# Two layers of attention and routed feed-forward on one core: sixteen small stores become one, and the order inside the row-maximum pairs

## The chip, the cores and the metric

The kernel runs on one core of a Trainium2 chip. The metric is the device time of one execution in microseconds (us). The kernel before took 4527.57 us, the median of three runs (4526.86 to 4528.15). A profile of one further execution stands beside them. In it the engines are called PE (matrix products), PEld (its weight loads), DVE (vector operations), ACT (activations), POOL (a second elementwise engine) and SP, whose queue issues most of the transfers between the chip's memory and the core's own.

## The reference

Two layers are applied twice in turn: full attention with 32 heads on 2048 rows of width 1024, then a feed-forward block that only the 8 rows with the highest router score pass through.

```python
def _A_ref(x, wqkv, wo):
    H = 32; Dh = D // H
    q, k, v = ...                       # x @ wqkv, split into heads of 32 columns
    scores = jnp.einsum("bhqd,bhkd->bhqk", q, k) * Dh ** -0.5
    p = _softmax(scores, axis=-1)
    o = jnp.einsum("bhqk,bhkd->bhqd", p, v)
    return o... @ wo

def _B_ref(x, w_r, w_gate, w_up, w_down):
    r = x @ w_r
    idx = jnp.argsort(-r, axis=-1)[:, :8]
    ...                                 # silu(x_sel @ w_gate) * (x_sel @ w_up) @ w_down, scaled by sigmoid(r_sel)
    return x + upd                      # the chosen rows are added back

x = A_x
x = x + _A_ref(_layernorm(x), A_wqkv, A_wo)
x = x + _B_ref(_layernorm(x), B_w_r, B_w_gate, B_w_up, B_w_down)
x = x + _A_ref(_layernorm(x), A_wqkv, A_wo)
x = x + _B_ref(_layernorm(x), B_w_r, B_w_gate, B_w_up, B_w_down)
```

The change lies in the softmax of the attention: in its row maxima and in its row sums.

## The kernel before, in words

Each layer has a stage of projections, an attention stage, and a stage with the output projection and the feed-forward block. The attention stage is cut into 32 *units*: 8 groups of 4 heads, and for each group 4 chunks of 512 queries (`QC`, line 23). A unit has 16 *steps*, one for each tile of 128 keys, so a layer's attention stage has 512 steps. The order of every engine's instructions is the order of the code (`manual_schedule`, line 101); only waits are put in by the builder.

**One step** (the loop at line 1298) issues on PE, in this order: the first pair of row-maximum products for a later unit (`pre_pair` with k = 0, line 1318), the score products of two head pairs (`scores`, line 775; ACT turns each result into exponentials at line 1260), the second pair (`pre_pair` with k = 1, line 1325), and the product of the step before with the values (`pv_step`, line 1154).

**Row maxima.** The softmax needs the maximum of each row ahead of its unit, so the products for it run 25 steps early (`LEAD`): step s works on row block s + 25. For a block, `pre_pair` forms products with four stretches of 512 keys in two pairs. Two heads lie in the two halves of the array's rows, so the two products of a pair, b = 0 and b = 1, go to different halves and to different PSUM banks `ps[0]` and `ps[1]`. They come from a pool of three banks (`ps_st`, line 108), out of which the row sums and their totals take a bank too. `jj`, the lowest bit of the block's number, says which of the two heads is done with *paired keys*: for that head the first product (k = 0) is with differences of keys (`DT`, read as `dt` in the profile), ACT keeps the positive part of it (line 739), and the second product (k = 1) is added and the maximum taken in one operation on DVE (line 741), so that one reduction covers 1024 keys. The other product of each pair, with plain keys, is reduced alone on DVE (line 743). `jj` changes from step to step: in one step the product with paired keys is b = 0, in the next b = 1. The products are issued with b = 0 first in both.

**Row sums.** The exponentials of the 16 key tiles of a unit are added up, partly by transfers that accumulate (line 1194), partly by POOL (line 1164). What is left is summed over the 128 rows in two ways. `sum_out` (line 1218) uses products with ones for the tiles named `DIRECT` and stores four rows (`sd`). For the accumulated rest, `turn` (line 1166) transposes 32-by-32 blocks and reduces them into a small tile `FOLD`, in eight operations spread over steps 8 to 15 of the next unit. Once in four units, in step 15, `total` (line 1179) adds the four partition groups with one product, transposes the result and stores it to the memory tensor `sd2` (called `se` in the profile). `sum_load` (line 1224) reads both tensors at the end of the layer. The last three units of a layer are not turned; their places in `sd2` are filled once, at the stage's start, by three stores of zeros (line 1253).

**The queue.** All loads and stores of this stage but the accumulating ones are issued by SP in the order of the code (`dma`, line 103, called from line 105 in the profile). After `total` of step 15 come, in steps 0 to 5 of the next unit: the store of the last unit's output (`oT`, line 1210, after DVE's copy at line 1208) and six query loads for the unit after next (`load_q`, line 703), one a step. The first four (`q<-qh`) carry what the row-maximum products read; these begin on that unit in step 7. After them come the stores of `sum_out` and, in two units of four, the keys of the next group. Three query tiles take turns.

Of the kernel before, what the change touches and what calls it, by code (L numbers as in the profile page):

```python
# [8 lines left out]
F32 = mybir.dt.float32  # L9
# [4 lines left out]
OP = mybir.AluOpType  # L14
AX = mybir.AxisListType
# [6 lines left out]
NG = H // 4  # L22
QC = 4
# [29 lines left out]
TURNED = NU - 3  # L53
# [23 lines left out]
def tile_kernel(ctx, tc, x, wqkv, wo, w_r, w_gate, w_up, w_down, out):  # L77
    nc = tc.nc
    sync, dve, act, pool, pe = nc.sync, nc.vector, nc.scalar, nc.gpsimd, nc.tensor
# [23 lines left out]
    def dma(out, in_):  # L103
        f = [a.bitcast(F32) if a.dtype == F32R else a for a in (out, in_)]
        sync.dma_start(f[0], f[1])  # L105

    def ps_st():
        return banks["now"][1].tile([128, 512], F32, name="st", bufs=1 if banks["wide"] else 3)

    def ps_pre():  # L110
        return psum.tile([128, 1024], F32, name="pre", bufs=2)

    def ps_pv():
        return psum.tile([128, 512], F32, name="pv")
# [12 lines left out]
    lanes = cons.tile([128, 32], F32, name="lanes")  # L127
# [540 lines left out]
    def layer(n, src, dst, prev=None, following=None):  # L668
# [7 lines left out]
        sd2 = dram.tile([NT, 4, NG, 128], F32, name=f"se{n}")  # L676
# [7 lines left out]
        KS, Q, V, NM, QP, DT = {}, {}, {}, {}, [], {}  # L684
# [27 lines left out]
        def half(h, slot):  # L712
            return slice(64 * (h % 2), 64 * (h % 2) + SLOT_ROWS[slot])

        def load_d(g, b, i):
            dma(DT[g % 2][64 * b:64 * b + 32, i, :].rearrange("p (c k) -> p c k", c=2),
                kd[g, 2 * b:2 * b + 2, 64 * i + 32 * b:64 * i + 32 * b + 32, :].rearrange("c p k -> p c k"))

        def pre_pair(u, r, k, side):

            qt, rest = divmod(r, 4)
            i, jj = divmod(rest, 2)
            g = u // QC
            if u not in NM:
                NM[u] = small.tile([128, 4, 4, 4], F32, name="nm", bufs=3)
            ps = [ps_st(), ps_st()]
            for b in range(2):
                rows, p = half(b, 0), ps[b]
                if b != jj:
                    keys = KS[g % 2][rows, i, 0, (2 * jj + k) * 512:(2 * jj + k + 1) * 512]  # L730
                elif k == 0:
                    keys = DT[g % 2][rows, i, :]
                else:
                    keys = KS[g % 2][rows, i, 0, jj * 1024:(jj + 1) * 1024].rearrange("p (c k) -> p c k", c=2)[:, :, 256:512]
                    p = p.rearrange("p (c k) -> p c k", c=2)
                pe.matmul(p, Q[u][rows, i, 0, qt * 128:(qt + 1) * 128], keys, start=True, stop=True, tile_position=(64 * b, 0))  # L736
            h = 2 * i + jj
            if k == 0:
                act.activation(side, ps[jj], AF.Relu)  # L739
            else:  # L740
                dve.tensor_tensor_reduce(side, ps[jj], side, 1.0, -3.0e38, OP.add, OP.max, NM[u][:, 0, h, qt:qt + 1])  # L741
            h = 2 * i + 1 - jj
            dve.tensor_reduce(NM[u][:, 1 + k, h, qt:qt + 1], ps[1 - jj], axis=AX.X, op=OP.max)  # L743
# [58 lines left out]
        with ExitStack() as pst:  # L802
# [249 lines left out]
            for k, (c, wb, i) in enumerate(steps):  # L1052
                b = k % 24
# [18 lines left out]
                j = k // 2 + 1  # L1072
# [7 lines left out]
                t = 4 * (c + 1) + at // 4  # L1080
# [41 lines left out]
        with sbuf(f"at{n}", bufs=2) as aw:  # L1122
# [5 lines left out]
            P, PV, ACC, TURN, FOLD = {}, {}, {}, {}, {}  # L1128
# [37 lines left out]
            def turn(u, k):  # L1166
                h, back = divmod(k, 2)
                if not back:
                    TURN[u] = aw.tile([128, 512], F32, name="turned", bufs=1)
                    dve.transpose(TURN[u], ACC[u][:, 512 * h:512 * h + 512])  # L1170
                    return
                if u % QC == 0 and h == 0:
                    FOLD[u // QC] = aw.tile([128, 4, 64], F32, name="fold", bufs=1)
                dve.tensor_reduce(FOLD[u // QC][:, u % QC, 16 * h:16 * h + 16], TURN.pop(u).rearrange("p (a c) -> p a c", c=32),
                                  axis=AX.X, op=OP.add)
                if h == 3:
                    ACC.pop(u)

            def total(u):
                if u % QC != QC - 1 and u != TURNED - 1:  # L1180
                    return
                g, m = u // QC, u % QC + 1
                p = ps_st()[0:32, 0:64 * m]
                pe.matmul(p, lanes, FOLD.pop(g)[:, 0:m, :].rearrange("p q c -> p (q c)"), start=True, stop=True, tile_position=(0, 0))
                t = aw.tile([128, 512], F32, name="sm", bufs=1)[0:32, 0:64 * m]
                dve.transpose(t, p)
                for q in range(m):
                    for h in range(4):
                        r = 16 * (h % 2)
                        dma(sd2[4 * q:4 * q + 4, h, g, :].rearrange("t (c r) -> t c r", r=32),  # L1190
                            t[r:r + 16, 64 * q + 32 * (h // 2):64 * q + 32 * (h // 2) + 32])

            def merge(u, a, b):
                pool.dma_start(P[u * NT + a], P[u * NT + b], accum_op=OP.add)  # L1194
# [33 lines left out]
            def recip(t, i):  # L1228
# [3 lines left out]
                dma(half_of(rd, i), t)  # L1232

            fns = {"add": acc_add, "merge": merge, "sum": sum_out, "turn": turn, "total": total}

            def emit(s, where):
# [13 lines left out]
            for i in range(2):  # L1250
                for b in range(2):
                    load_d(0, b, i)
            for t in range(TURNED % QC, QC):
                dma(sd2[4 * t:4 * t + 4, :, NG - 1, :].rearrange("t h c -> (t h) c"), DT[0][32:48, 0, 0:128])
            wop = None
            def half_step(s, i, third=False):
                if i == 0:
# [40 lines left out]
            for s in [*range(threes), *range(threes, NS, 3), *range(NS, NS + 14)]:  # L1298
# [14 lines left out]
                if pr:  # L1313
                    side = aw.tile([128, 512], F32, name="first", bufs=1) if s % NT != 1 or pr[0] >= PLAIN else None
                    if pr[0] < PLAIN:
                        pre_mm(*pr, 0, False, side=side)
                    else:
                        pre_pair(*pr, 0, side)
# [3 lines left out]
                if pr and pr[0] < PLAIN:  # L1322
                    pre_mm(*pr, 1, False)
                elif pr:
                    pre_pair(*pr, 1, side)
                t = s - 1 if s < NS - LEAD else s - 2
# [18 lines left out]
        if True:  # L1345
# [81 lines left out]
            for t in range(NT - 2 if n else NT):  # L1427
                oh, ol = OT.pop(t)
                p = ps_pre()
# [7 lines left out]
                if True:  # L1437
                    for k, l, r, a in products:
                        if first_stage and k == 2 and (t - CT, a) in ((0, 7), (1, 0), (1, 6), (2, 0), (2, 6), (3, 0)):
                            next(first_stage, None)  # L1440
                        for bl in halves:
                            pe.matmul(p[:, bl], l[:, a, :], r[a][:, bl], start=(k == 0 and a == 0),  # L1442
                                      stop=(k == 2 and a == KD - 1))
# [47 lines left out]
        if n:  # L1491
# [3 lines left out]
            p = [[waste[:, h] for h in halves], [ps_st(), ps_pv()]]  # L1495
# [72 lines left out]
            for i in range(2):  # L1568
                t = NT - 2 + i
# [11 lines left out]

    x3 = tuple(dram.tile([rows, D], F32, name=f"x3{i}") for i, rows in enumerate((CUT + 8, S - CUT)))
    list(layer(0, x, x3, following=lambda ffn: layer(1, x3, out, prev=ffn)))


# [24 lines left out]
```

## Time and profile before

| | |
|---|---|
| median of three runs | 4527.57 us |
| profiled execution | 4530.56 us |
| its span, first to last instruction | 4528.8 us |
| mean granted PE clock | 0.982 |
| busy PE, DVE, ACT, POOL | 97%, 68%, 63%, 72% |
| stores `se<-sm` of the turned sums | 232, 2 KB each |
| row-maximum products (line 736) | 2880 with plain keys, 960 with paired keys |

Busy time is the union of an engine's instructions; PE's ends are modelled, so a busy PE is not PE at its peak. A row of a time table has the start in us from the span's start, the length in us from the first to the last of the instructions merged into it, the engine, the line, the operation, and what it writes and reads; in brackets stands the idle time ahead of it and what ended it. "SPq" and the like are the queue of an engine, which issues transfers and waits.

### The profile page before, as it was taken

The page shows a single profiled execution, that of the slowest core. Times are in us where ns is not written, and L with a number is a line of the kernel's source. Part 1 is how long each engine was busy: PE and PEld are TensorE (multiplying, and loading weights), DVE is VectorE, ACT ScalarE, POOL GpSimd, SP SyncE. Part 2 cuts the span into 40 slices and gives each one's busy share as a digit, 9 for nine tenths or more (in the row PEclk, how much of TensorE's full clock was granted, in tenths as well). Part 3 has the DMA queues.
Part 4 walks back from the last instruction along what each step waited for, and adds up shares of the span by engine and source line. Part 5 has one row for each costly group of instructions (what it writes and reads, how often), then busy time and mean ns, then how long its engine had stood idle before and what let it go on. Part 6 is the DMA issues. An engine that isn't in the chain of part 4 may idle for free.

```text
span 4528.8 us, 75535 instructions
## 1 busy us (share of the span) xinstructions
PE 4383.9 (97%) x28255; PEld 2646.1 (58%) x28255; DVE 3059.5 (68%) x5605; ACT 2867.5 (63%) x3447; POOL 3268.6 (72%) x1367
## 2 busy tenths in 40 slices
PE   9999999999999999999999999999999999999998
PEld 7888755445445454458877786545454454544584
DVE  3322588778878787786522226878787888887863
ACT  3322299889888888870222223989898898988600
POOL 5554399889899898835634443989898898988252
PEclk9999999999999999999999999999999999999999
DMA  6977498888898988769699774988988888887698
GB/s 222 271 242 225 134 200 190 178 187 187 177 199 173 196 185 179 165 161 248 182 312 314 251 211 135 197 186 185 195 186 178 185 186 185 191 178 158 167 284 329
DMA packets 366189, 918.69 MB, mean 203 GB/s; under 512 B 52700, under 2 KB 188476, under 8 KB 309486
## 3 DMA queue, kind: packets, MB, share of 16 engines
q0 software_dynamic: 53312, 384.39, 42.7%
q1 hardware_dynamic: 295198, 490.07, 35.8%
q10 hardware_dynamic: 17312, 39.40, 3.0%
q8 instruction: 222, 3.64, 0.3%
q14 instruction: 145, 1.19, 0.1%
HBM read 395.35 MB, written 134.67 MB: 117 GB/s over the span
## 4 chain that ended last, share of the span: by engine, by line
PE 88%; DMA 6%; DVE 2%; issue 1%; SPq 1%; POOL 1%; ACT 0%; POOLq 0%; ACTq 0%; DVEq 0%
PE pv L1154 22%; PE pre L775 21%; PE st L932 16%; PE st L736 15%; PE pre L932 6%; PE pre L1442 5%; DMA q<-qh 2%; SPq L105 1%; PE st L1203 1%; DMA wraw<-in_A_wqkv_dram 1%; PE pre L757 1%; PE pv L932 1%; DMA ord<-rd 0%; PE pv L567 0%; PE third L775 0%
## 5 line engine op out<-in xcount | busy, mean ns | idle before, releaser
L1164 POOL TENSOR_TENSOR acc<-acc,P 128x2048 f32<-128x2048 f32 x420 | 2054.6, 4892 | 9.4
L1260 ACT ACTIVATE P<-pre 128x1024 f32<-128x1024 f32 x2016 | 1954.9, 1023 | 25.6 <-PE pre L775 23.8
L743 DVE TENSOR_REDUCE nm<-st 128x1 f32<-128x512 f32 x1920 | 1320.8, 688 | 159.9 <-PE st L736 134.7
L775 PE MATMUL pre<-q,ks 64*128 64x512 f32 (+1 forms) x8064 | 1136.4, 397 | 1.7 <-ACT P L1260 1.7
L1154 PE MATMUL pv<-P,v 128*32 128x512 f32 x8192 | 1097.6, 610 | 0.3 <-DMA v<-vd 0.3
L736 PE MATMUL st<-ks,q 64*128 64x512 f32 x2880 | 929.3, 451 | 0.1
L775 PEld LDWEIGHTS pre<-q,ks 64*128 64x128 f32 (+1 forms) x8064 | 779.2, 188 | 162.6 <-ACT P L1260 27.8
L741 DVE CUSTOM_DVE_ANT_0 first<-st,first 128x512 f32<-128x512 f32 x960 | 664.1, 692 | 304.2 <-PE st L736 278.2
L739 ACT ACTIVATE first<-st 128x512 f32<-128x512 f32 x960 | 575.9, 600 | 382.0 <-PE st L736 379.6
L736 PEld LDWEIGHTS st<-ks,q 64*128 64x128 f32 x2880 | 515.3, 186 | 474.1 <-DVE nm L741 375.8
L736 PE MATMUL st<-dt,q 64*128 64x512 f32 x960 | 481.6, 502 | 111.1 <-DMA q<-qh 86.9
L1194 POOL DMA_DIRECT2D P<-P x366 | 367.5, 1004 | 297.9 <-PE st L736 223.7
L736 PEld LDWEIGHTS st<-dt,q 64*128 64x128 f32 x960 | 177.2, 185 | 515.0 <-ACT P L1260 340.4
L947 DVE TENSOR_TENSOR lo<-st,hi 128x512 fp32r<-128x512 f32 x128 | 88.4, 691 | 511.3 <-ACT hi L946 453.1
L832 POOL TENSOR_TENSOR ohl<-wraw,ord 128x2048 fp32r<-128x2048 f32 (+1 forms) x54 | 222.3, 4122 | 242.2 <-ACT ord L827 211.5
L946 ACT CAST hi<-st 128x512 fp32r<-128x512 f32 x128 | 75.3, 588 | 441.2 <-PE st L932 347.3
L832 POOL TENSOR_TENSOR wl<-wraw,wh 128x2048 fp32r<-128x2048 f32 (+1 forms) x54 | 223.1, 4134 | 171.4 <-ACT wh L831 153.8
L1154 PEld LDWEIGHTS pv<-P,v 128*32 128x32 f32 x8192 | 163.9, 108 | 267.8 <-issue 261.1
L1164 POOL TENSOR_TENSOR acc<-P 128x2048 f32<-128x2048 f32 x62 | 311.6, 5026 | 0.1
L181 POOL TENSOR_TENSOR rs<-mv,eps_c 128x1 f32<-128x1 f32 x64 | 26.8, 419 | 288.1 <-DVE mv L179 288.1
L1442 PE MATMUL pre<-woh,ohl 128*128 128x512 f32 x960 | 223.9, 390 | 2.8 <-DVE pre L1476 1.9
L1373 ACT CAST ohl<-ord 128x1024 fp32r<-128x1024 f32 x32 | 33.6, 1051 | 273.7 <-DMA ord<-rd 93.6
(421 smaller groups left out, 5311.6 us busy)
## 6 DMA issues: line engine op xcount, KB each, us to landing
P<-P POOLq DMA_DIRECT2D x366, 1024.0 KB, 9.1
wraw<-in_A_wqkv_dram SPq DMA_DIRECT2D x96, 1024.0 KB
q<-qh SPq DMA_DIRECT2D x256, 128.0 KB
ks<-kh SPq DMA_DIRECT2D x112, 256.0 KB
fw<-in_B_w_down_dram SPq DMA_DIRECT2D x17, 1024.0 KB
vd<-vn SPq DMA_DIRECT2D x32, 512.0 KB
qh<-hi SPq DMA_DIRECT2D x64, 256.0 KB
ql<-lo SPq DMA_DIRECT2D x64, 256.0 KB
```

Source lines behind the costliest of these rows:

```text
L736: pe.matmul(p, Q[u][rows, i, 0, qt * 128:(qt + 1) * 128], keys, start=True, stop=True, tile_position=(64 * b, 0))
L739: act.activation(side, ps[jj], AF.Relu)
L741: dve.tensor_tensor_reduce(side, ps[jj], side, 1.0, -3.0e38, OP.add, OP.max, NM[u][:, 0, h, qt:qt + 1])
L743: dve.tensor_reduce(NM[u][:, 1 + k, h, qt:qt + 1], ps[1 - jj], axis=AX.X, op=OP.max)
L775: pe.matmul(p[:, b * 512:(b + 1) * 512], KS[(u // QC) % 2][rows, i, slot, kt * 128:(kt + 1) * 128], Q[u][rows, i, slot, :], start=(slot == ...
L832: pool.tensor_tensor(wl[:, sl], raw[:, sl], wh[:, sl].bitcast(F32), op=OP.subtract)
L932: pe.matmul(p, *pair(a, l, r), start=(a == 0 and k == 0), stop=(a == KD - 1 and k == 2))
L1154: pe.matmul(PV[u][32 * h:32 * h + 32, :], V[g, kt // 4][:, kt % 4, 32 * h:32 * h + 32], P[s][:, h, :], start=(kt == 0), stop=(kt == NT - 1 ...
L1164: (dve if on_dve else pool).tensor_tensor(o, a, P[u * NT + k].rearrange("p h c -> p (h c)"), op=OP.add)
L1194: pool.dma_start(P[u * NT + a], P[u * NT + b], accum_op=OP.add)
L1260: act.activation(P[s][:, 2 * i:2 * i + 2, :].rearrange("p h c -> p (h c)"), p, AF.Exp, scale=SCALE)
L1442: pe.matmul(p[:, bl], l[:, a, :], r[a][:, bl], start=(k == 0 and a == 0), stop=(k == 2 and a == KD - 1))
```

## The change

In `pre_pair` the two products of a pair are issued in the order `jj`, `1 - jj`: the product with paired keys first. Nothing else of the function changes; where `jj` is 0 the order is what it was.

For the turned sums, `FOLD` becomes a tile of 256 columns in another order, into which the reduction writes with a stride, so that after the total and its transposition each of 32 rows holds two pieces of 128 sums as they lie in memory. `total` then stores the sums of four units with one transfer of 32 rows by 2 pieces of 512 bytes in place of sixteen of 16 rows by 128 bytes. The last total of a layer, which has one unit, also takes all 256 columns; the fold tile of that group is set to zero first, and the three stores of zeros at the start of the stage go.

```diff
-            for b in range(2):
+            for b in (jj, 1 - jj):
                 rows, p = half(b, 0), ps[b]
...
                 if u % QC == 0 and h == 0:
-                    FOLD[u // QC] = aw.tile([128, 4, 64], F32, name="fold", bufs=1)
-                dve.tensor_reduce(FOLD[u // QC][:, u % QC, 16 * h:16 * h + 16], TURN.pop(u).rearrange("p (a c) -> p a c", c=32),
-                                  axis=AX.X, op=OP.add)
+                    FOLD[u // QC] = aw.tile([128, 256], F32, name="fold", bufs=1)
+                    if u // QC == NG - 1:
+                        dve.memset(FOLD[u // QC], 0.0)
+                i, j = divmod(u % QC, 2)
+                out = FOLD[u // QC].rearrange("p (i c j t h) -> p i j h t c", i=2, c=4, j=2, t=4)[:, i, j, h]
+                dve.tensor_reduce(out, TURN.pop(u).rearrange("p (t c r) -> p t c r", t=4, c=4), axis=AX.X, op=OP.add)
...
-                g, m = u // QC, u % QC + 1
-                p = ps_st()[0:32, 0:64 * m]
-                pe.matmul(p, lanes, FOLD.pop(g)[:, 0:m, :].rearrange("p q c -> p (q c)"), start=True, stop=True, tile_position=(0, 0))
-                t = aw.tile([128, 512], F32, name="sm", bufs=1)[0:32, 0:64 * m]
+                p = ps_st()[0:32, 0:256]
+                pe.matmul(p, lanes, FOLD.pop(u // QC), start=True, stop=True, tile_position=(0, 0))
+                t = aw.tile([128, 512], F32, name="sm", bufs=1)[0:32, 0:256]
                 dve.transpose(t, p)
-                for q in range(m):
-                    for h in range(4):
-                        r = 16 * (h % 2)
-                        dma(sd2[4 * q:4 * q + 4, h, g, :].rearrange("t (c r) -> t c r", r=32),
-                            t[r:r + 16, 64 * q + 32 * (h // 2):64 * q + 32 * (h // 2) + 32])
+                dma(sd2[:, :, u // QC, :].rearrange("(i r) h c -> (r h) i c", i=2), t.rearrange("p (i c) -> p i c", i=2))
...
-            for t in range(TURNED % QC, QC):
-                dma(sd2[4 * t:4 * t + 4, :, NG - 1, :].rearrange("t h c -> (t h) c"), DT[0][32:48, 0, 0:128])
```

## Prediction

> **What bounds the kernel now.** I read the page's busy table and the costliest groups first, then the waits, then time tables of single stretches. In the groups and waits the last columns are busy us, mean ns, and the idle time of the engine with its releaser; a wait has its total, its count and its longest.
>
> ```profile
> span 4528.8 us, 75535 instructions
> PE 4383.9 (97%) x28255; PEld 2646.1 (58%) x28255; DVE 3059.5 (68%) x5605; ACT 2867.5 (63%) x3447; POOL 3268.6 (72%) x1367
> L736 PE MATMUL st<-dt,q 64*128 64x512 f32 x960 | 481.6, 502 | 111.1 <-DMA q<-qh 86.9 <-DMA sd<-sm 24.2
> PE st L736 <- DMA q<-qh: 86.9, 11, 8.3
> ```
>
> PE is busy for 97%, so only two things can pay: an idle stretch of PE, or a product that PE runs late. The first stands in the third row: PE is idle for 111.1 us ahead of the paired-key products, and a transfer ends it. The waits split that into 11 waits on query loads and 3 put down to a small store; their longest is about 8 us, so these are 14 long stops, not a cost spread over 960 products. The change touches both the queue behind those stops and the order of those products.
>
> **Why PE stops.** First the queue that issues the loads (SP), start and length in us, around one stop; then PE there. The second pair of fences is the unit before, which has no stop.
>
> ```profile
> 960.62 16.04 SPq L105 DMA_DIRECT2D se<-sm  x16
> 976.76 0.90 SPq L105 DMA_DIRECT2D oT<-o  x1
> 977.76 4.28 SPq L105 DMA_DIRECT2D q<-qh  x4
> ```
> ```profile
> 978.63 1.04 PE L1203 MATMUL st<-P,ones 128*32 128x512 f32 x8
> 987.23 0.76 PE L736 MATMUL st<-dt,q 64*128 64x512 f32 x1 [7.55 <-DMA q<-qh]
> ```
> ```profile
> 920.15 0.37 SPq L105 DMA_DIRECT2D oT<-o  x1
> ...
> 921.32 3.46 SPq L105 DMA_DIRECT2D q<-qh  x4
> ```
> ```profile
> 934.82 1.04 PE L1203 MATMUL st<-P,ones 128*32 128x512 f32 x8
> 935.79 0.50 PE L736 MATMUL st<-dt,q 64*128 64x512 f32 x1
> ```
>
> The sixteen stores of the turned sums hold SP for 16.04 us. Behind them stand the store of the previous unit's output and the four query loads without which the pair products of the unit after next cannot start. Those loads are issued until 982.04, and PE, done with its sums at 979.67, starts again at 987.23. One unit earlier the same loads are out at 924.78 and PE goes from its sums to the next pair in 0.97 us. The sixteen stores come once in four units, so 7 times in each of 2 layers: 14.
>
> The whole price is read from windows that reach from one unit's sums to the next. Columns: length; busy time of PE, weight loads, DVE, ACT, POOL; granted clock; DMA share; GB/s. The first three rows are the first, the last and the sum of the 14 windows with a stop; then the same of 14 windows without one.
>
> ```profile
> 793.91:847.92 54.01, 46.19 (x332) 23.47 (x328) 38.04 (x79) 39.30 (x49) 41.90 (x15) 0.91 0.84 185
> ...
> 4146.51:4200.90 54.39, 46.16 (x334) 23.56 (x330) 38.15 (x80) 39.30 (x49) 42.03 (x15) 0.91 0.68 142
> sum 755.83, PE 644.64 PEld 327.33 DVE 532.32 ACT 550.48 POOL 586.56; mean PE 46.05 PEld 23.38 DVE 38.02 ACT 39.32 POOL 41.90
> ```
> ```profile
> 847.92:891.29 43.37, 43.37 (x333) 22.26 (x329) 37.86 (x79) 39.25 (x49) 42.00 (x15) 1.00 0.80 166
> ...
> sum 606.93, PE 606.93 PEld 311.12 DVE 530.22 ACT 549.37 POOL 588.77; mean PE 43.35 PEld 22.22 DVE 37.87 ACT 39.24 POOL 42.06
> ```
>
> (755.83 - 606.93) / 14 = 10.64 us for each stop, 148.9 us in all. That is more than the idle 111.1 us, and the clock says why:
>
> ```profile
> 987.20:992.80 5.60, 5.51 (x22) 2.48 (x22) 2.11 (x5) 2.54 (x3) 0.00 (x0) 0.50 0.25 70
> 992.80:998.40 5.60, 5.60 (x46) 3.02 (x46) 5.00 (x10) 4.85 (x6) 2.29 (x2) 1.00 0.25 49
> ```
>
> After the stop PE works 5.6 us at clock 0.50 (22 matmuls, then 46 in the same time), which loses about 2.8 us. The Trainium skill (TensorE: Matmul & The Clock Gate, What's actually happening) has the clock halved after an idle window of about 3.4 us and freed after about 3.4 us of work. By that figure a stop would lose 1.7 us in place of 2.8 and the 14 some 15 us less, as an estimate; the trace shows 5.6 us, and I go by it.
>
> **Part 1, one transfer for sixteen.** SP loses 15 of 16 issues. What is left of the 16.04 us is one issue: 1.00 us by their mean, 1.07 by the query loads' (4 in 4.28). So SP is free by about 961.7. Next is the output store, which needs DVE's copy:
>
> ```profile
> 963.14 0.68 DVE L1208 COPY o<-pv 128x512 f32<-128x512 f32 x1
> ```
>
> It can go at 963.8. From that store's start to the last query load the undisturbed unit took 924.78 - 920.15 = 4.6 us, so the loads are out at 968.4. In the stop PE ran 5.2 us after the last one (982.04 to 987.23); with that they have landed at 973.6, and PE asks at 979.67: 6 us to spare, against 935.79 - 924.78 - 5.2 = 5.8 in the undisturbed unit. The stop goes whole, and with it the half clock: -148.9 us. The loads that the stop used to push back now share the DMA engines with key loads and merges; that is a rival below.
>
> The Trainium skill speaks against this part: DMA: Bandwidth & Descriptors, under Issuing engines are not separate DMA queues, calls the sequencer's time to issue a transfer usually small beside the transfer. The row above has 16 issues of 2 KB at 1.00 us each, so here it is not small; were the page right here, the stop would have another cause (third rival).
>
> The other edits: the reduction writes its 16 sums with a stride. The nearest pair of rows is a DVE operation with permuted operands and its straight twin:
>
> ```profile
> L1174 DVE TENSOR_REDUCE fold<-turned 128x16 f32<-128x512 f32 x232 | 156.9, 676 | 0.0
> L847 DVE TENSOR_SCALAR xt<-xt,mv,rs 128x1024 f32<-128x1024 f32 x20 | 17.9, 897 | 34.7 <-POOL rs L182 34.6
> L853 DVE TENSOR_SCALAR xt<-xt,mv,rs 128x1024 f32<-128x1024 f32 x12 | 11.0, 915 | 42.1 <-POOL rs L182 42.1
> ```
>
> 915 against 897 is 2%, so 0 to 14 ns on each of 232, at most 3 us if all were exposed; DVE has 43.35 - 37.87 = 5.5 us free in a unit that hides them, and I take 0. The two clears of the fold tile, the wider last total and the six filling stores that go are one or two operations per layer, below 1 us either way: 0.
>
> **Part 2, the order of the pair.** Two steps in a row: one where the paired-key product is first already (dt at 1249.90), one where it is second (dt at 1252.51). PE, its weight loads, ACT and DVE:
>
> ```profile
> 1249.90 0.49 PE L736 MATMUL st<-dt,q 64*128 64x512 f32 x1
> ...
> 1250.24 1.09 PE L775 MATMUL pre<-q,ks 64*128 64x512 f32 x8
> 1251.17 0.41 PE L736 MATMUL st<-ks,q 64*128 64x512 f32 x2
> 1251.51 1.06 PE L1154 MATMUL pv<-P,v 128*32 128x512 f32 x8
> 1252.50 0.49 PE L736 MATMUL st<-ks,q 64*128 64x512 f32 x1
> 1252.51 0.49 PE L736 MATMUL st<-dt,q 64*128 64x512 f32 x1
> ...
> 1253.77 0.51 PE L736 MATMUL st<-ks,q 64*128 64x512 f32 x2
> 1254.21 1.07 PE L1154 MATMUL pv<-P,v 128*32 128x512 f32 x8
> 1255.20 0.50 PE L736 MATMUL st<-dt,q 64*128 64x512 f32 x1
> ```
> ```profile
> 1250.93 0.33 PEld L736 LDWEIGHTS st<-ks,q 64*128 64x128 f32 x2
> ...
> 1253.54 0.42 PEld L736 LDWEIGHTS st<-ks,q 64*128 64x128 f32 x2
> ```
> ```profile
> 1250.43 0.60 ACT L739 ACTIVATE first<-st 128x512 f32<-128x512 f32 x1 [0.22 <-PE st L736]
> ...
> 1253.07 0.60 ACT L739 ACTIVATE first<-st 128x512 f32<-128x512 f32 x1 [0.16 <-PE st L736]
> ```
> ```profile
> 1252.33 1.40 DVE L743 TENSOR_REDUCE nm<-st 128x1 f32<-128x512 f32 x2
> ```
>
> The first kind of step takes 2.60 us, the second 2.70, and the 0.10 lies between the step's second pair and pv: 1251.17 to 1251.51 against 1253.77 to 1254.21. The weight loads tell what is late. One load takes 0.18, so the second load starts at 1251.08 in the one step and at 1253.78 in the other. 1251.08 is 0.05 after ACT's end (1251.03); 1253.78 is 0.05 after DVE's second reduction ends (1253.73). So the second product of the second pair takes the bank that the step's first pair gave back first: that of its first-issued product, read by ACT in one step and by DVE in the other. The three score banks are handed out when the program is built. If that rule holds, issuing dt first gives the second kind of step ACT's bank too: ACT's reading starts 0.53 after the pair (as at 1250.43), ends at +1.13, and the second pair's loads can go at +1.18, as in the first kind. DVE's later end then holds nobody. Gain 0.10 at most on 480 steps (30 units x 8 x 2 layers), 48 us; I take 0.093, since both loads of the pair then stand behind that wait and not just the second: -44.5 us. What the gain uncovers is POOL: busy 42.06 of 43.35 us, and the unit falls to about 42.6.
>
> **Sum.** 4528.8 us is the span; the profiled execution took 4530.56. 4530.56 - 148.9 - 44.5 = 4337.2. It lay 3.0 us above the median of the three runs (4527.57), so the median to expect is 4334.
>
> **Rivals.**
> 1. *A new bound takes part of it* (0.12). A window with a stop has a DMA share of 0.85, some 45.8 us of transfer time, to be packed into 42.6 us; POOL has 0.5 us left. Against it: in no window shown is a wait put down to a merge or a key load. If the DMA engines set the pace there, 14 x 3.2 = 45 us come back: up to 4379.
> 2. *The banks do not follow the issue order* (0.11). Then the second kind of step still waits for DVE, whose product is now issued second. ACT starts 0.57 after the pair where its product is second and 0.53 where it is first, so DVE would be 0.04 later: +19 us on 480 steps in place of -44.5, 4334 + 44 + 19 = 4397. From below the loss is the 0.01 between the two issues, 5 us. The Trainium skill (TensorE: Matmul & The Clock Gate, The cost: per-tile semaphore tail) puts a second increment about 26 ns behind the first, an estimate of 12 us here.
> 3. *The stop is not SP's* (0.04): it stays, and only part 2 is gained, 4483. For it speaks that 3 of the 14 stops are put down to another transfer; against it, that all 14 come once in four units.
> 4. *Slower* (0.03). The swapped order breaks the overlap of the two row groups. Eight score products take 0.93 us between the pairs (1250.24 to 1251.17), 0.23 per two that overlap. One after the other would add 0.23 to each of 960 swapped pairs, 221 us, in place of part 2's gain: 4334 + 44 + 221 = 4599. It decides from 149 / 960 = 0.155 us per pair. Against it: in every pair shown both start within 0.01 us.
> 5. *Nothing changes* (0.02): 4528.
>
> **How the numbers follow.** My forecast has 0.68 with a range of its own of 4324 to 4346 (part 2 between 34 and 48 us, some us for the rest). Cases 1 and the forecast make 0.80, so the range is 4322 to 4380. A change under 0.2% (9 us) could not be told from none here. Faster: the forecast and rivals 1 to 3, 0.95, less 0.02 for mishaps that I don't see, 0.93; same 0.03; slower 0.04.
>
> **What would show it.** Right: no idle time over 1 us of PE ahead of the dt products, one se store of about 1 us in four units, the clock at 1.00 through both attention stages, units of about 42.6 us, and both kinds of step at 2.60. Part 1 is wrong if query loads still end waits of PE; part 2 is wrong if odd steps stay at 2.70 or reach 2.74 with the second weight load behind DVE's end; units at 43 with POOL never idle would be rival 1.

## The result and the profile after

The changed kernel took 4340.76 us (4336.97 to 4348.58, four runs) beside 4527.86 us (4526.86 to 4528.24) of the kernel before: a ratio of 0.959, with a 95% interval of 0.957 to 0.961. That is 187.1 us less; the forecast was 193.6 less (4527.57 - 4334). In a later comparison, on another chip and beside other kernels, it took 4349.02 us (4344.87 to 4351.77) against 4529.46, a ratio of 0.960 (0.959 to 0.962), or 180.4 us less; so differences of some 8 us between medians of different comparisons mean nothing here. One execution of a kernel further below, the one with the stores in the gap, took 6616.10 us at a granted clock of 0.579 and is left out of its numbers.

The page of the changed kernel's profiled execution, which was the longest of its four runs (4348.58 us), and its costliest groups:

```profile
span 4346.8 us, 75763 instructions
PE 4307.6 (99%) x28255; PEld 2612.5 (60%) x28255; DVE 3045.8 (70%) x5607; ACT 2880.2 (66%) x3447; POOL 3270.6 (75%) x1367
L736 PE MATMUL st<-dt,q 64*128 64x512 f32 x960 | 476.3, 496 | 0.0
L736 PE MATMUL st<-ks,q 64*128 64x512 f32 x2880 | 874.3, 432 | 2.0 <-issue 2.0
```

The 111.1 us of idle time ahead of the paired-key products are gone. A time table of the changed kernel shows why, at the place of a former stop: first SP's queue, then PE.

```profile
944.17 0.30 SPq L105 DMA_DIRECT2D se<-sm  x1
947.34 0.38 SPq L105 DMA_DIRECT2D oT<-o  x1
947.82 3.21 SPq L105 DMA_DIRECT2D q<-qh  x4
```
```profile
961.87 1.04 PE L1201 MATMUL st<-P,ones 128*32 128x512 f32 x8
962.84 0.50 PE L736 MATMUL st<-dt,q 64*128 64x512 f32 x1
```

The one store holds SP for 0.30 us, the query loads are out at 951.03, and PE goes from its sums to the next pair in 0.97 us, as it did before only in units without a stop.

The windows with a former stop, from sums to sums as in the prediction: the first, one to come back to, and the sum of all 14.

```profile
790.80:833.38 42.58, 42.58 (x332) 21.84 (x328) 37.46 (x77) 39.41 (x49) 41.64 (x15) 1.00 0.98 212
...
3629.78:3676.34 46.56, 44.53 (x332) 22.66 (x328) 37.85 (x79) 39.58 (x49) 42.01 (x15) 0.96 0.96 203
...
sum 601.50, PE 599.47 PEld 308.05 DVE 528.20 ACT 552.62 POOL 586.65; mean PE 42.82 PEld 22.00 DVE 37.73 ACT 39.47 POOL 41.90
```

601.50 us in place of 755.83. Eleven of the 14 windows now last 42.5 to 42.6 us (the last one of each layer 43.4), but the DMA share (the second last number) has risen, in the first one from 0.84 to 0.98, and one window has a stop of its own.

Last, two steps in a row of the changed kernel. The second (from 1226.67) is of the kind that had the paired-key product second. PE, the weight loads, ACT and DVE:

```profile
1224.07 0.50 PE L736 MATMUL st<-dt,q 64*128 64x512 f32 x1
...
1225.12 0.32 PEld L736 LDWEIGHTS st<-ks,q 64*128 64x128 f32 x2
...
1226.51 1.42 DVE L743 TENSOR_REDUCE nm<-st 128x1 f32<-128x512 f32 x2
1226.67 0.49 PE L736 MATMUL st<-dt,q 64*128 64x512 f32 x1
...
1227.20 0.60 ACT L739 ACTIVATE first<-st 128x512 f32<-128x512 f32 x1 [0.18 <-PE st L736]
1227.71 0.33 PEld L736 LDWEIGHTS st<-ks,q 64*128 64x128 f32 x2
...
1229.27 0.50 PE L736 MATMUL st<-dt,q 64*128 64x512 f32 x1
```

Both steps take 2.60 us. In the second, one load taking 0.18, the second load starts at 1227.86: 0.06 after ACT's end (1227.80) and before DVE's second reduction ends (1227.93). DVE no longer holds the pair.

### The profile page after: what moved, and what is told of

It reads as the page before. It is cut to its first block, busy times and chain, and to the rows that moved or that the text cites. A ratio compares the mean times of both kernels' runs of the same rounds, so it can differ in the third digit from the quotient of the medians.

```text
span 4346.8 us, 75763 instructions
## 1 busy us (share of the span) xinstructions
PE 4307.6 (99%) x28255; PEld 2612.5 (60%) x28255; DVE 3045.8 (70%) x5607; ACT 2880.2 (66%) x3447; POOL 3270.6 (75%) x1367
## 4 chain that ended last, share of the span: by engine, by line
PE 93%; DMA 3%; DVE 1%; issue 1%; POOL 1%; ACT 0%; SPq 0%; POOLq 0%; ACTq 0%; DVEq 0%
PE pv L1154 23%; PE pre L775 22%; PE st L932 17%; PE st L736 15%; PE pre L1438 6%; PE pre L932 5%; PE st L1201 1%; PE pv L567 1%; DMA wraw<-in_A_wqkv_dram 1%; PE pre L757 1%; PE pv L932 1%; DMA ord<-rd 0%; PE third L775 0%; DMA P<-P 0%; PE st L607 0%
## 5 line engine op out<-in xcount | busy, mean ns | idle before, releaser
L775 PE MATMUL pre<-q,ks 64*128 64x512 f32 (+1 forms) x8064 | 1123.1, 395 | 2.4 <-ACT P L1256 2.4
L736 PE MATMUL st<-ks,q 64*128 64x512 f32 x2880 | 874.3, 432 | 2.0 <-issue 2.0
L775 PEld LDWEIGHTS pre<-q,ks 64*128 64x128 f32 (+1 forms) x8064 | 770.5, 186 | 159.9 <-ACT P L1256 32.1
L736 PEld LDWEIGHTS st<-ks,q 64*128 64x128 f32 x2880 | 487.9, 185 | 46.0 <-issue 2.3
```

Source lines behind the costliest of these rows:

```text
L775: pe.matmul(p[:, b * 512:(b + 1) * 512], KS[(u // QC) % 2][rows, i, slot, kt * 128:(kt + 1) * 128], Q[u][rows, i, slot, :], start=(slot == ...
```

## The experiments

### Each part alone

Here the order inside the pairs is the old one and only the sixteen stores become one:

```diff
-            for b in (jj, 1 - jj):
+            for b in range(2):
```

> The changed kernel with the old order inside the pairs: only the sixteen stores become one. Theory (the 14 stops are the sixteen issues on SP, the odd steps wait for a bank that DVE gives back): the stops go, odd steps stay at 2.70 us, undisturbed units at 43.35. Time 4528 - 149 = 4379 us, plus some 6 us of what the changed kernel showed to be left over, so 4379 to 4386. Rival A (the two parts share their gain, since a faster step uses up the time that query loads have): without the faster steps nothing is left over, 4379 or a little less. Rival B (the stops are not SP's): near 4528.

Here the stores are the old ones and only the order is changed:

```diff
-            for b in range(2):
+            for b in (jj, 1 - jj):
```

> The kernel before with the paired-key product first and the sixteen stores as they were. Theory: the 14 stops stay, and since steps are shorter PE asks up to 1 us earlier for query loads that come no earlier, so part 2's gain in the 14 former-stop windows is lost in them: odd steps at 2.60, undisturbed units at 42.54, stops 0.2 to 1 us longer. 480 odd steps by 0.10 would be -48, of which up to 10 us go to the longer stops: 4480 to 4492 us. Rival (banks do not follow the issue order): 4528 to 4547, odd steps at 2.70 to 2.74.

The one transfer alone took 4387.66 us (4384.55 to 4391.02), a ratio of 0.969 (0.967 to 0.971) and 140 us less than 4527.71 before. The order alone took 4496.96 us (4496.23 to 4497.61), 0.993 (0.991 to 0.995) and 30.8 us less. The parts do not add up: 140.1 + 30.8 = 170.8 us, and together they bring 187 (180 in the later comparison). The windows with a stop say where most of the rest is. Their sums, of the one transfer alone and of the order alone:

```profile
sum 608.03, PE 608.03 PEld 311.50 DVE 530.99 ACT 549.33 POOL 586.57; mean PE 43.43 PEld 22.25 DVE 37.93 ACT 39.24 POOL 41.90
```
```profile
sum 754.34, PE 637.44 PEld 324.09 DVE 529.32 ACT 553.71 POOL 585.75; mean PE 45.53 PEld 23.15 DVE 37.81 ACT 39.55 POOL 41.84
```

The transfer takes 755.83 - 608.03 = 147.8 us out of these 14 windows (the prediction: 148.9). The order takes 1.5 us out of them where 14 shorter units should bring 14 x 0.79 = 11 (units without a stop went from a mean of 43.38 us with the one transfer alone to 42.59 in the changed kernel). PE asks earlier for the same query loads and waits longer for them. The groups of that kernel show it:

```profile
L736 PE MATMUL st<-dt,q 64*128 64x512 f32 x960 | 480.6, 501 | 116.1 <-DMA q<-qh 108.2 <-DMA sd<-sm 7.8
```

116.1 us in place of 111.1. The other part of the loss is in the clock: in two of the 14 windows the granted clock was 0.88 and 0.87, where all windows of the kernel before had 0.90 or 0.91. So a part of the gain by the order can be had only once the stops are gone. With them gone it is 4387.66 - 4340.76 = 46.9 us between medians of two comparisons (38.6 with the changed kernel's later median); 60 units of 0.79 us make 47.

### Which pair of the step decides

The changed kernel, with the paired-key product first in one pair of a step alone:

```diff
-            for b in (jj, 1 - jj):
+            for b in ((jj, 1 - jj) if k == 0 else (0, 1)):
```

> The changed kernel with the paired-key product first in the first pair of a step (k = 0) alone; the second pair has the old order. Theory (the second pair's later product takes the bank that the first pair's first-issued product gave back): the first pair's order sets it, so the whole of part 2 is kept: odd steps at 2.60, about 4341 us like the changed kernel. Rival A (the second pair's own order sets who waits): odd steps at 2.70, 4380 to 4386. Rival B (both count): near 4361.

```diff
-            for b in (jj, 1 - jj):
+            for b in ((0, 1) if k == 0 else (jj, 1 - jj)):
```

> The changed kernel with the paired-key product first in the second pair of a step (k = 1) alone; the first pair has the old order. Theory: the first pair still issues the plain product first in odd steps, so the second pair's second load waits for DVE's reduction of it as before: odd steps at 2.70, 4380 to 4386 us. Rival A (the second pair's own order sets it): odd steps at 2.60, about 4341. Rival B: near 4361.

First pair alone: 4347.32 us (4344.45 to 4351.75), 0.960 (0.959 to 0.962). Second pair alone: 4386.88 us (4383.88 to 4387.60), 0.969 (0.967 to 0.970), the time of the kernel with the one transfer alone. A step of the former second kind in each; first pair alone, then second pair alone:

```profile
1228.03 1.42 DVE L743 TENSOR_REDUCE nm<-st 128x1 f32<-128x512 f32 x2
1228.19 0.50 PE L736 MATMUL st<-dt,q 64*128 64x512 f32 x1
...
1229.24 0.32 PEld L736 LDWEIGHTS st<-ks,q 64*128 64x128 f32 x2
...
1230.80 0.50 PE L736 MATMUL st<-dt,q 64*128 64x512 f32 x1
```
```profile
1232.10 0.50 PE L736 MATMUL st<-ks,q 64*128 64x512 f32 x1
...
1232.65 0.68 DVE L743 TENSOR_REDUCE nm<-st 128x1 f32<-128x512 f32 x1
1232.68 0.60 ACT L739 ACTIVATE first<-st 128x512 f32<-128x512 f32 x1 [0.17 <-PE st L736]
1233.16 0.41 PEld L736 LDWEIGHTS st<-ks,q 64*128 64x128 f32 x2
...
1234.82 0.49 PE L736 MATMUL st<-dt,q 64*128 64x512 f32 x1
```

With the first pair turned the step takes 2.61 us and its second load starts at 1229.38, before DVE is done (1229.45). With only the second pair turned it takes 2.72, and the second load starts at 1233.39, 0.06 after DVE's reduction of this step's first product (1233.33) and 0.11 after ACT (1233.28). So it is the first pair's order that decides for whom the second pair waits, as the prediction's rule had it; the second pair's own order brings nothing that can be told.

### The same sixteen stores at another place

To tell the place in SP's queue from the transfers themselves, the old sixteen stores were kept and issued later, with the changed order inside the pairs (the sums of that unit use the tile of the output meanwhile):

```diff
-                        dma(sd2[4 * q:4 * q + 4, h, g, :].rearrange("t (c r) -> t c r", r=32),
+                        late.append((sd2[4 * q:4 * q + 4, h, g, :].rearrange("t (c r) -> t c r", r=32),
...
                     f(*args)
+                if kt == 9:
+                    while late:
+                        dma(*late.pop(0))
```

> The old sixteen stores with the paired-key product first; SP issues the sixteen stores behind step 9 of the unit after the total, when the six query loads, the stores of sums and the row maxima are out, in place of ahead of them. Number, size and form of the stores stay. Theory (the stops come from the place of sixteen issues in SP's queue, ahead of the query loads): no stops, PE not idle ahead of the paired-key products, 4340 to 4352 us, like the changed kernel. Rival (the sixteen small transfers themselves slow the DMA engines, and the query loads with them): the stops stay, about 4497 us, or come back later in the unit.

It took 4503.98 us (4500.87 to 4507.96), 0.995 (0.993 to 0.996): about as slow as the order alone, as the rival had it. But the stops were not where they had been. Its time table, at the old place, then the queue, then a unit later:

```profile
974.41 1.04 PE L1203 MATMUL st<-P,ones 128*32 128x512 f32 x8
975.39 0.50 PE L736 MATMUL st<-dt,q 64*128 64x512 f32 x1
...
1026.77 0.76 PE L736 MATMUL st<-dt,q 64*128 64x512 f32 x1 [8.77 <-DMA q<-qh]
```
```profile
989.33 16.07 SPq L105 DMA_DIRECT2D se<-sm  x16
...
1010.75 3.26 SPq L105 DMA_DIRECT2D q<-qh  x4
```

My place was badly chosen: SP, busy with key loads and row maxima, came to the stores at 989.3 and issued the next unit's query loads from 1010.75 on. The stop had moved with the sixteen issues, to the next query loads behind them. So they were moved once more, to a unit of the group in which SP has no keys to load:

```diff
-                if kt == 9:
+                if kt == 8 and (u % QC == 2 or u == NU - 3):
```

> The old sixteen stores with the paired-key product first, as in the run that put them behind step 9 of the unit after the total; there SP was also busy with key loads, came to the stores at 989.3, was held to 1005.4, and the stops came back one unit later behind the next unit's query loads (issued from 1010.8). Now the stores wait for the unit without key loads (step 8 of the third unit of a group), where SP has some 25 us free. Theory (a stop comes where sixteen issues stand ahead of query loads in SP's queue, and only there): no stops at all, 4340 to 4355 us. Rival (the sixteen transfers themselves cost PE its loads): stops of about 10 us, 4490 to 4505.

This took 4350.05 us (4341.03 to 4350.40, three runs), a ratio of 0.960 (0.959 to 0.962): the changed kernel's time, with all sixteen stores. Its groups, and its queue:

```profile
L736 PE MATMUL st<-ks,q 64*128 64x512 f32 x2880 | 872.2, 432 | 2.6 <-DMA q<-qh 1.6 <-DVE nmc L783 0.9
L736 PE MATMUL st<-dt,q 64*128 64x512 f32 x960 | 475.5, 495 | 0.0
```
```profile
1014.86 14.26 SPq L105 DMA_DIRECT2D se<-sm  x16
...
1032.61 3.95 SPq L105 DMA_DIRECT2D q<-qh  x4
```

SP is still held for 14.26 us, but nothing that is due waits behind it, and of the 14 stops none is left; the 1.6 us on `q<-qh` in the first row are one wait in another unit, like the one that the changed kernel has (below). The stops were a matter of order in one queue, not of the transfers.

### Sixteen issues of the new form

```diff
-                dma(sd2[:, :, u // QC, :].rearrange("(i r) h c -> (r h) i c", i=2), t.rearrange("p (i c) -> p i c", i=2))
+                for r in range(16):
+                    dma(sd2[:, :, u // QC, :].rearrange("(i r) h c -> r h i c", i=2)[r // 2, 2 * (r % 2):2 * (r % 2) + 2],
+                        t[2 * r:2 * r + 2, :].rearrange("p (i c) -> p i c", i=2))
```

> The changed kernel with its one transfer of the sums cut into sixteen of two rows by two pieces of 512 bytes, at the same place: sixteen issues again, but 4 descriptors in each in place of 16. Theory (an issue costs its time whatever it carries): SP is held for 9 to 16 us as before, the stops return: at 1.00 us an issue 4490 to 4500 us, at 0.6 us some 9.6 us of hold against 6 us to spare, stops of 3 to 4 us with little or no half clock, 4380 to 4420. Rival (the many short descriptors are what costs): near 0.3 us an issue as for the single transfer, 5 us of hold, no stops, 4340 to 4350.

It took 4450.40 us (4448.56 to 4455.79), 0.983 (0.981 to 0.984): between the cases. Queue and PE of this kernel at one place, and the sum of the 14 windows:

```profile
954.26 11.79 SPq L105 DMA_DIRECT2D se<-sm  x16
...
967.01 5.08 SPq L105 DMA_DIRECT2D q<-qh  x4
```
```profile
975.28 0.47 PE L736 MATMUL st<-dt,q 64*128 64x512 f32 x1 [2.27 <-DMA q<-qh]
978.29 0.76 PE L736 MATMUL st<-ks,q 64*128 64x512 f32 x1 [2.54 <-DMA q<-qh]
```
```profile
sum 704.19, PE 636.27 PEld 322.62 DVE 530.39 ACT 553.84 POOL 586.29; mean PE 45.45 PEld 23.04 DVE 37.89 ACT 39.56 POOL 41.88
```

That is 0.74 us an issue: the form took 4 us off the 16, and the number, from sixteen to one, the other 11.5. So the number of issues counts most, the form less. SP is held for 11.8 us, and 2.27 + 2.54 = 4.8 us of them show as idle PE; so 7 us found room, where the prediction had 6 us to spare. With the half clock behind it a stop costs about (704.19 - 601.50) / 14 = 7.3 us.

### What the forecast left over

The window at 3629.78 above has 4.0 us too many. In the time table of the changed kernel, queue and PE:

```profile
3615.73 2.39 SPq L105 DMA_DIRECT2D q<-qh  x4
```
```profile
3630.75 0.50 PE L736 MATMUL st<-dt,q 64*128 64x512 f32 x1
3633.27 0.46 PE L736 MATMUL st<-ks,q 64*128 64x512 f32 x1 [2.03 <-issue]
```

The product of the other head started 15.2 us after the last of these loads had been issued. The profile names no releaser here. In a second profile of the changed kernel it does, at another unit: loads issued until 3100.62, PE idle for 2.29 us until 3116.27, again 15.7 us:

```profile
3097.99 2.63 SPq L105 DMA_DIRECT2D q<-qh  x4
...
3116.27 0.47 PE L736 MATMUL st<-ks,q 64*128 64x512 f32 x1 [2.29 <-DMA q<-qh]
```

Two kernels were made to test this, and the changed kernel was run beside them. One issues the four query loads ahead of the output store, which waits for DVE's copy:

```diff
-                    loads.extend((load_q, u + 2, i) for i in range(len(q_loads)))
+                    loads.extend((lambda: None,) for i in range(4))
+                    loads.extend((load_q, u + 2, i) for i in range(4, len(q_loads)))
...
+                if s % NT == 0 and s // NT + 2 < NU:
+                    for i in range(4):
+                        load_q(s // NT + 2, i)
                 if s == 2:
                     pv_step(0)
                 if s not in (1, NS - LEAD) and 0 <= t < NS:
                     pv_step(t)
```

> The changed kernel, but the four query loads with the high halves leave in step 0 of the unit, ahead of the output store, which waits for DVE's copy; the key loads keep their steps. What the changed kernel did not gain of the forecast (4341 in place of 4334, runs from 4337 to 4349) was to be looked for in query loads that land late: one of them, issued at about 3617.5, let PE go at 3633.2 only. Theory: issued some 3 us earlier, they are never late; no PE idle ahead of the products of step 7, 4334 to 4339 us and a spread of runs below 3 us. Rival (the loss lies in merges that land late, or in the output store and copy that now come later): 4338 to 4346 with the same spread.

The other leaves out four of the sixteen loads of a group's keys from the third group on (the scores then use older keys, so its result is another):

```diff
         def load_k(g, h, i, sl=slice(0, S)):
+            if g > 1 and i == 1:
+                return
```

> The changed kernel without the loads of the low halves of the keys from the third group on (4 of 14 loads of key data per group, 1 MB less; the scores then use the low halves of an earlier group, so the result is another). Theory (what is left over comes from full DMA engines: the mean share in the attention stage is 0.9 and more): query loads and merges land earlier, 4333 to 4338 us, spread below 3 us. Rival (the left over is not the DMA engines'): 4338 to 4346, same spread.

> The changed kernel itself, for its spread on the same chip: every theory expects a median of 4337 to 4345 us and runs between 4336 and 4350.

| on one chip | us | ratio to before (95%) |
|---|---|---|
| changed kernel | 4349.02 (4344.87 to 4351.77) | 0.9602 (0.9589 to 0.9615) |
| query loads first | 4339.51 (4334.99 to 4341.03) | 0.9578 (0.9565 to 0.9592) |
| fewer key loads | 4340.29 (4337.85 to 4348.31) | 0.9584 (0.9571 to 0.9597) |

With the query loads first the slowest run lies below the changed kernel's fastest beside it, and neither row of its products shows a wait:

```profile
944.15 4.95 SPq L105 DMA_DIRECT2D q<-qh  x4
949.20 0.40 SPq L105 DMA_DIRECT2D oT<-o  x1
```
```profile
L736 PE MATMUL st<-ks,q 64*128 64x512 f32 x2880 | 872.6, 432 | 0.0
L736 PE MATMUL st<-dt,q 64*128 64x512 f32 x960 | 475.6, 495 | 0.0
```

Its span in the profiled execution is 4335.2 us, 193.6 less than that of before (4528.8); the forecast was 193.4 (148.9 + 44.5). So the late query loads are gone, and this version beats the changed kernel by 9.5 us in this comparison; against the first comparison's 4340.76 it cannot be told apart. They are not the whole of it either: the first profiled execution of the changed kernel is 11.6 us longer than this one, of which 4.0 lie in the window at 3629.78, 1.2 in another unit in which PE waits for no query load, and 4.3 between and after the two attention stages, where it waits for none either. Two things fell short. The spread of runs stayed at 6 us (3 us when the kernel was run once more). And leaving out key loads helped by about as much in the median but with one run at 4348, so that the key loads' share in it is likely but not shown.

In one more kernel, with the query loads first, the total itself was moved as well, three steps later:

```diff
-        ev += [...] + [(TURN_AT + 7, "mid", 5, "total", ())]
+        ev += [...] + [(TURN_AT + 10, "mid", 5, "total", ())]
...
-                for back in (1, 0):
+                for back in (2, 1, 0):
```

> The query loads ahead of the output store as before, and the total of the turned sums three steps later (behind the value products of step 2 of the next unit), so that its weight load no longer waits for the last reduction (0.30 us) in step 15. The step with the total took 0.41 us more than its neighbours, the one behind it 0.14, 14 times. Theory: 0.2 to 0.4 us of each go, 3 to 6 us below the kernel with the query loads first alone. Rival (the product and its bank cost the same anywhere): no difference.

> The changed kernel with the four query loads ahead of the output store, once more beside the others: 4335 to 4341 us by every theory.

4345.70 us (4341.17 to 4351.35) with the later total, 4341.17 us (4339.18 to 4342.19; 0.9583, 0.9570 to 0.9596) without it: no gain, rather a loss. The step with the total was 0.40 us longer than its neighbours at the new place too, and the one behind it 0.14. The price is the same at both places; whether the product or its bank makes it was not tried.

## Why the prediction was right, and what it missed

**The stops and their price.** Right. All 14 went with the one transfer, also without the other part, and the 14 windows lost 147.8 us where 148.9 were predicted. That SP's queue was the cause is shown by the stores in the gap: sixteen stores, 14.26 us of hold, no stop. The third rival (the stop is not SP's) falls. The Trainium skill (DMA: Bandwidth & Descriptors, Issuing engines are not separate DMA queues) says that the sequencer's time to start a transfer is usually small beside the transfer. The prediction read this as speaking against part 1, which went too far: the sentence compares one issue with its own transfer, and no profile here gives the time that one small store took; the stop came from sixteen issues in a row, 16.04 us, ahead of a load that was due.

**One issue.** Mis-sized, with little effect: 0.30 us, not 1.00.

**"6 us to spare."** This step failed in part. The issue times were about right: the query loads were out 11.8 us before PE asked (951.03 against 962.84), and 968.4 against 979.67 had been forecast. The 5.2 us that they needed to land, taken from a stop, were not: with the DMA share at 0.98 in place of 0.84 the product began up to 15.7 us after the last of them was issued. That this brought back one stop in each of two profiles, and not more, was not worked out ahead; there the forecast had some luck, and the clock was not at 1.00 throughout, as it wanted. It looks like the first rival's mechanism (DMA engines that set the pace) at a tenth to a fifth of its price: 4.0 us in the one profile and at most 9.5 us in the medians beside the kernel with the query loads first, where the rival had 45. Its sum put 45.8 us of transfer time into such a window; the undisturbed window at 961.87 holds 0.98 x 42.54 = 41.7. The same section of the Trainium skill says that transfers of all queues share the same 16 DMA engines and interleave, which agrees with this. The one transfer alone came out at 140 us in the medians and 146 us in its profiled execution; what its slower executions lost has no profile.

**The order of the pair.** Right in the rule and nearly in size: 46.9 us measured on top of the one transfer (38.6 with the later median), 44.5 predicted. Steps of both kinds take 2.60 us, and only the first pair's order matters, as "the bank of the first-issued product" says. The second rival (banks do not follow the issue order) falls: its odd steps would have stayed at 2.70. The fourth (broken overlap) falls too, since both products of a pair still start within 0.01 us. What the prediction did not say is that this gain depends on the other part: in the 14 windows with a stop it is worth 1.5 us in place of 11, so alone it brings 30.8.

**Edits costed at nothing.** The strided reduction takes 678 ns against 676:

```profile
L1178 DVE TENSOR_REDUCE fold<-turned 128x16 f32<-128x512 f32 x232 | 157.4, 678 | 0.1
```

**Units.** 42.6 us were forecast, and most units without the total came out at 42.54; POOL, with 41.9 of them, did not become the bound.

## What to carry to other kernels

Many small stores cost by their number on the queue that issues them, and the price is paid by whatever load stands behind them; either make them one, or put them where no load that someone waits for follows. After a stall is gone, look at what was resting in it: here the DMA engines went from 0.84 to 0.98 busy, and issuing the loads with the nearest due time first took the waits on them away. Where products share few banks, as here, the reader of the first-issued product sets when the next pair can go, so issue first the one whose reader is done first.

## What the runs showed of the hardware

**An issue on SP is slow from about 1.5 to 6 us behind the issue of an accumulating transfer.** The 232 small stores of the kernel before lasted from 0.58 to 1.62 us:

```profile
L105 SPq DMA_DIRECT2D se<-sm x232: 582/1004/1618, 775.9 to 4186.0; - x116
```

Sorted by the time since POOL had last issued a merge (`P<-P`, 1 MB), the mean of one issue in ns was:

| us since the merge's issue | 0 to 1 | 1 to 2 | 2 to 3 | 3 to 4 | 4 to 5 | 5 to 6 | 6 to 7 | 7 to 8 |
|---|---|---|---|---|---|---|---|---|
| old stores, kernel before | 665 | 888 | 1245 | 1278 | 1258 | 1071 | 584 | 583 |
| old stores, in the gap | 593 | 814 | 1262 | 1264 | 1272 | 969 | 590 | 582 |
| sixteen of the new form | 363 | 405 | 804 | 1010 | 1034 | 702 | 339 | 251 |

So the 1.00 us of the prediction was a mean over two prices, 0.58 and 1.26, and SP's hold hung on how the stores met the merges (16.04 us at one place, 14.26 in the gap). The one store of the changed kernel was issued 1.2 to 2.4 us behind a merge, at the edge of the slow stretch, and took 0.30 each time; what it would cost inside is not shown. A merge lands 9.1 us after its issue in the median, when issues have long been cheap again, so it is not simply that a merge is under way. That the merge is the cause is read from the times alone; no run left the merges out.

**A stop of 2 us can bring the half clock, but need not.** The windows after the 2.03 us of idle PE at 3633 in the changed kernel, then the one after 2.35 us of idle PE, until 3319.43, in the kernel with sixteen issues of the new form (the clock is the third last number):

```profile
3633.20:3635.20 2.00, 1.93 (x15) 1.34 (x19) 1.02 (x2) 0.90 (x1) 1.92 (x2) 1.00 1.05 220
3635.20:3638.60 3.40, 3.40 (x18) 1.81 (x12) 2.40 (x6) 2.09 (x4) 3.10 (x1) 0.50 0.80 192
3638.60:3642.00 3.40, 3.40 (x28) 1.52 (x30) 2.75 (x6) 2.96 (x5) 1.36 (x2) 1.00 0.02 4
```
```profile
3319.40:3330.00 10.60, 10.57 (x81) 5.60 (x83) 9.45 (x20) 9.11 (x11) 9.41 (x4) 1.00 0.82 175
```

In the first case the half clock came 2 us after PE had started again and lasted 3.4 us; in the second, with the longer stop, it did not come. What decides is not shown. The Trainium skill (TensorE: Matmul & The Clock Gate, What's actually happening) has an idle window of about 3.4 us before the half clock and about 3.4 us of work until it ends. The first case went into it after less; the time until its end agrees.
